# Sparse attention and a gated feed-forward on one core: at most three of the opening's transfers in flight

## The chip, the core and the metric

One NeuronCore of a Trainium2 chip runs the whole program. The metric is device time in microseconds (us) of one execution; the figure of record is the median of several runs. Times in a profile count from the start of its span.

## The reference

Attention over 8 batches, 8 heads, 576 positions and 64 values a head, then a feed-forward of 4608 tokens, 512 wide inside and out, 2048 hidden:

```python
mask_local = (rel >= 0) & (rel < 32)
mask_strided = (rel >= 0) & (pos[None, :] % 32 == pos[:, None] % 32)
scores = np.where(masks, q @ k.T / np.sqrt(D), -1e9)      # heads 0-3 local, 4-7 strided
attn = softmax(scores)
x = (attn @ v) laid out as (tokens, heads * D)
h = x @ w_in
sp = np.maximum(h, 0.0) + np.log1p(np.exp(-np.abs(h)))
g = h * erf(sp)
out = g @ w_out
```

## The kernel before

Inputs come in a layout made for the chip: for each batch and pair of heads one block of queries and keys (`qk_loc` or `qk_str`, for local and strided heads) and one of values (`v_loc`, `v_str`). The weights are of eight bytes a number and are loaded as pairs of 32-bit words (tile `words`, 512 KB a block of 128 by 512); VectorE joins the words to 32-bit floats in three steps (L628, L635, L641: `bits0`, `bits1`, `bits2`), ScalarE rounds them to a high part (L646) and VectorE keeps the rest (L649). There are 16 blocks of `w_in` and 16 of `w_out`. The feed-forward multiplies high and low parts (L678 into `h`, L750 into `o`), and its gate is worked out by ScalarE (L686) and VectorE (L683, L713, L719).

`heads` makes one pair of heads: two loads or more (L378 to L389), scores on TensorE (L400, and L413 adds the mask there), their maximum on VectorE (L436), the exponential on ScalarE, the sum and its inverse on VectorE (L481, L490, L491), the product on GpSimd (L498), a transpose on TensorE (L507) and the product with the values (L526). The eight pairs of the first two batches go first, and all but one of these borrow the space of weight blocks that come later (`home`), so their queries, keys and values are loaded in two parts, and those weight blocks are loaded when the pair is through. The other batches are made in between the feed-forward's work.

Nothing of the order is left to a scheduler. Each operation is an `Op` with an engine, a duration and a key; `Plan.order` plays them through and writes one fixed order for each engine, which `tc.keep_in_program_order` keeps. All loads and the first stores are issued by SyncE (engine `sp` in the plan), in that one order. The plan reckons with code fetches of TensorE, one in every 254 of its instructions:

```python
BLOCK, FIRST, FETCH = 254, 68, (4.0, 5.8)
late = max(0.0, fetched + self.FETCH[fetched < dma] - at)
```

The semaphores are put in by the framework: a transfer waits for its data's buffer to be free, and eight completion semaphores are used in turn, so that a transfer also waits for the landing of the eighth ahead of it.

The first 60 transfers of SyncE are: for the eight pairs of heads of the first two batches their loads, the masks (`con`) and the identity (`ident`), two loads of the third batch, and 30 of the 32 weight blocks, between 64 and 640 KB each. Numbers of transfers in this document count in the order of issue; 1 and 2 are the queries and keys of the first pair, 3 is `con`, 4 and 5 queries and keys of the second pair, 6 the first weight block, 7 and 8 values of the first pair (512 and 128 KB), 9 `ident`, 10 values of the second pair, 11 queries and keys of the third pair, 15 and 20 weight blocks of `w_in`.

Of the kernel before, what the change touches and what calls it, by code (L numbers as in the profile page):

```python
# [27 lines left out]

PRO = 36
SLOT = 4.6  # L30
BACKLOG = 1.1130116
FT = (31.6335, -135.614, 224.291, 52.3709, -149.741, 22.9733, 45.4447, 151.185, -55.3448, 2.76331, -71.5147, 15.0393)
KI = 6.0
# [124 lines left out]
class Plan:  # L158
# [14 lines left out]
    def add(self, eng, dur, key, emit, after=(), new=(), use=(), earliest=0.0):  # L173
        op = Op(eng, dur, key, emit, after, new, use, earliest)
        self.ops.append(op)
        return op
# [24 lines left out]
    def order(self):  # L201
# [5 lines left out]
        while left:  # L207
            best = None
            for e in self.ENGINES:
                can = [(o, n, self._ready(o, live)) for n, o in enumerate(queue[e][: self.WINDOW])]  # L210
                floor = max(free[e], dma - BACKLOG) if e == "sp" else free[e]
                port = held.get({"dve": "pool", "pool": "dve"}.get(e), 0.0)
# [54 lines left out]
def attention_moe(  # L267
# [39 lines left out]
    def buf(pool, tag, shape, name, dtype=F32):  # L307
        def make():
            return pools[pool].tile(shape, dtype, tag=tag, name=name, bufs=bufs[tag])

        return Buf(tag, make)
# [8 lines left out]
    def act(n, fixed=0.093):  # L320
        return fixed + n / 1200.0
# [343 lines left out]
    def ftile(k, c, f, first_f, last_f, ready):  # L665

        v0 = PRO + SLOT * k
        ph = buf("ps_h", "h", [P, 512], f"h_{k}")
# [73 lines left out]
        for t in range(NTT):  # L742
# [19 lines left out]
            if f == last_f:  # L762
# [12 lines left out]

                o = add("act", act(DM, 0.06), v0 + 2.5 * SLOT + 0.7 + 0.2 * t, evac, [o], [ob], [po])
                if first_f == 0:
# [30 lines left out]
    for f in range(0, DF, SW):  # L808
        for c in range(NCC):
            i = len(w1)  # L810
            rows, sl = slice(c * P, (c + 1) * P), slice(f, f + SW)
            op, pair = weight(i, w_in, rows, sl, KW[i // 8][i % 8])
            w1.append(op)
            win.append(pair)
    for f in range(NFC):
        rows, sl = slice(f * P, (f + 1) * P), slice(0, DM)
        op, pair = weight(NFC + f, w_out, rows, sl, KW[2 + f // 8][f % 8])
# [18 lines left out]
    for b in range(B):  # L836
        p2 = b // 2
        for i, hp in enumerate((0, 1, 2, 3)):
            keys = KP[4 * b + i]
            if p2 == 0:  # L840
                banks, home, act_sum, pool_norm = PAIRS[4 * b + i]
                done, o_s, o, loads = heads(
                    b, hp, keys, [], pe_mask=True, pool_norm=pool_norm, act_sum=act_sum, banks=banks, home=home, own=True
                )
# [22 lines left out]
    w, run = warm("o2")  # L867
    first = plan.add("pe", 0.217, -10.0, run, o_con, [w])
    plan.filler = (first, warm, ("o2", "o1", "o0", "ps"), mm1_first[6])
    for op in plan.order():  # L870
        for x in op.new:
            x.tile = x.make()
        for ins in op.emit():
            tc.keep_in_program_order(ins)


def _layout(q, k, v):
# [87 lines left out]
```

## Time and profile before

| | |
|---|---|
| median of 3 runs | 933.93 us (932.69 to 934.51) |
| the profiled execution | 933.05 us, span 931.3 us |
| busy: TensorE, VectorE, ScalarE, GpSimd | 909.7, 686.7, 653.4, 60.9 us |
| chain that ended last | TensorE 90%, VectorE 4%, ScalarE 3% |
| DMA, whole span | 68.86 MB, 74 GB/s |

PE is TensorE, PEld its weight loads, DVE VectorE, ACT ScalarE, POOL GpSimd, SPq the issue of transfers by SyncE. In a timeline row the first number is the start, the second the length; square brackets hold the idle time of the engine ahead of the instruction and what ended it, "issue" being nothing that the profile knows. In a row of busy times by stretch each engine has its busy us and the count of instructions (x), in the order PE, PEld, DVE, ACT, POOL, and then TensorE's granted clock, the DMA engines' busy share and their GB/s. Queue q1 carries SyncE's transfers, q8 and q14 carry code.

### The profile page before, as it was taken

To read this page: it belongs to the slowest core of one execution; us is meant where nothing else is said; L and a number is where in the kernel's file an instruction comes from. 1 tells how busy PE (TensorE), PEld (TensorE's weight loads), DVE (VectorE), ACT (ScalarE), POOL (GpSimd) and SP (SyncE) were. 2 spreads that over 40 slices of the span, in tenths; PEclk is the share of its full clock that TensorE was granted. 3 is DMA by queue.
4 is the path that set the end of the run, shared out by engine and by line. 5 is a ranking of instruction groups with operands and counts; after the bars stand their busy time and mean duration, and the time that the engine had idled before them with its cause. 6 is when DMAs were issued, how large, how long until landed. Compare 5 with 4: busy or idle time off the path is not lost.

```text
span 931.3 us, 20134 instructions
## 1 busy us (share of the span) xinstructions
PE 909.7 (98%) x8166; PEld 809.6 (87%) x8169; DVE 686.7 (74%) x1352; ACT 653.4 (70%) x1476; POOL 60.9 (7%) x59
## 2 busy tenths in 40 slices
PE   5789999999999999999999999999999999999998
PEld 4678888898888889988888899998898899999997
DVE  5999999996757766669886876667876666666664
ACT  5687887887776767667666666766766766766765
POOL 2200012110101100001110100000100000000000
PEclk9799999999999999999999999999999999999999
DMA  9994124321313010013312300002300200000000
GB/s 336 391 362 154 62 57 73 61 34 48 78 58 86 30 64 35 27 57 105 99 56 92 124 17 1 34 1 73 135 1 30 70 1 1 34 1 0 34 1 35
DMA packets 23421, 68.86 MB, mean 74 GB/s; under 512 B 2592, under 2 KB 3232, under 8 KB 23328
## 3 DMA queue, kind: packets, MB, share of 16 engines
q1 hardware_dynamic: 20736, 62.86, 18.9%
q0 software_dynamic: 2592, 4.72, 3.6%
q8 instruction: 64, 1.05, 0.5%
q14 instruction: 29, 0.24, 0.1%
HBM read 53.41 MB, written 14.16 MB: 73 GB/s over the span
## 4 chain that ended last, share of the span: by engine, by line
PE 90%; DVE 4%; ACT 3%; issue 1%; DMA 1%; SPq 0%; POOL 0%; ACTq 0%; POOLq 0%
PE h L678 41%; PE o L750 40%; PE s L400 3%; PE x L526 3%; PE t L507 2%; PE s L526 1%; DMA qk<-qk_loc 1%; ACT b L686 1%; DVE a L683 1%; DVE b L683 1%; ACT a L686 1%; PE s L507 1%; DVE glo L719 1%; ACT sm L472 0%; DVE h L713 0%
## 5 line engine op out<-in xcount | busy, mean ns | idle before, releaser
L750 PE MATMUL o<-pair,ghi 128*128 128x512 f32 x1152 | 361.4, 395 | 0.2 <-ACT ghi L716 0.2
L678 PE MATMUL h<-xhi,pair 128*128 128x384 f32 x1536 | 302.4, 339 | 0.6 <-DVE glo L719 0.6
L678 PEld LDWEIGHTS h<-xhi,pair 128*128 128x128 f32 x1536 | 271.4, 188 | 16.5 <-DVE glo L719 2.6
L686 ACT ACTIVATE b<-b 128x384 f32<-128x384 f32 x384 | 200.4, 522 | 77.2 <-DVE b L683 73.8
L750 PEld LDWEIGHTS o<-pair,ghi 128*128 128x128 f32 x1152 | 209.8, 188 | 32.4 <-ACT ghi L716 0.7
L750 PE MATMUL o<-pair,glo 128*128 128x512 f32 x576 | 224.8, 390 | 0.0
L683 DVE SCALAR_TENSOR_TENSOR a<-h,a 128x384 f32<-128x384 f32 x192 | 106.3, 553 | 83.3 <-ACT a L686 82.8
L678 PE MATMUL h<-xlo,pair 128*128 128x384 f32 x768 | 164.4, 336 | 0.0
L686 ACT ACTIVATE a<-h 128x384 f32<-128x384 f32 x192 | 93.5, 487 | 100.9 <-PE h L678 100.2
L683 DVE SCALAR_TENSOR_TENSOR a<-a,h 128x384 f32<-128x384 f32 x192 | 105.5, 549 | 68.9 <-ACT b L686 68.9
L713 DVE TENSOR_TENSOR h<-b,h 128x384 f32<-128x384 f32 x192 | 107.0, 557 | 46.2 <-ACT b L686 45.8
L678 PEld LDWEIGHTS h<-xlo,pair 128*128 128x128 f32 x768 | 136.0, 188 | 0.0
L750 PEld LDWEIGHTS o<-pair,glo 128*128 128x128 f32 x576 | 108.1, 188 | 23.7 <-DVE glo L719 0.3
L686 ACT ACTIVATE a<-a 128x384 f32<-128x384 f32 x192 | 100.3, 523 | 26.6 <-DVE a L683 26.1
L719 DVE TENSOR_TENSOR glo<-h,ghi 128x384 fp32r<-128x384 f32 x192 | 105.7, 550 | 11.7 <-ACT ghi L716 10.2
L716 ACT CAST ghi<-h 128x384 fp32r<-128x384 f32 x192 | 90.5, 471 | 29.1 <-DVE h L713 15.1
L683 DVE SCALAR_TENSOR_TENSOR b<-b,a 128x384 f32<-128x384 f32 x192 | 108.7, 566 | 1.0
L686 ACT ACTIVATE b<-a 128x384 f32<-128x384 f32 x192 | 101.0, 526 | 4.4
L498 POOL TENSOR_TENSOR sm<-sm,r 128x768 f32<-128x768 f32 (+3 forms) x36 | 45.0, 1249 | 435.3 <-DVE r L491 330.9
L436 DVE TENSOR_REDUCE mx<-s 128x12 f32<-128x768 f32 (+3 forms) x37 | 28.8, 784 | 10.6 <-PE s L413 10.3
L766 ACT COPY ob<-o 128x512 f32<-128x512 f32 x54 | 31.0, 588 | 2.7 <-PE o L750 2.2
L526 PEld LDWEIGHTS x<-pt,v 64*64 64x64 f32 x1392 | 24.4, 135 | 6.9 <-issue 4.4
(49 smaller groups left out, 511.4 us busy)
## 6 DMA issues: line engine op xcount, KB each, us to landing
out<-ob SPq DMA_DIRECT2D x36, 256.0 KB, 2.0
v<-v_loc SPq DMA_DIRECT2D x13, 640.0 KB, 4.1
words<-w_in SPq DMA_DIRECT2D x16, 512.0 KB, 8.6
words<-w_out SPq DMA_DIRECT2D x16, 512.0 KB, 9.1
qk<-qk_loc SPq DMA_DIRECT2D x13, 592.0 KB, 3.8
qk<-qk_str SPq DMA_DIRECT2D x12, 608.0 KB, 3.8
v<-v_str SPq DMA_DIRECT2D x16, 384.0 KB, 3.3
out<-ob POOLq DMA_DIRECT2D x18, 256.0 KB, 4.6
```

What stands on the lines that cost most here:

```text
L436: yield nc.vector.tensor_reduce(out=mx[:, parts[i], :units], in_=wide(of(s, i)), axis=mybir.AxisListType.X, op=ALU.max)
L498: yield (nc.gpsimd if pool_norm else nc.vector).tensor_tensor(out=d, in0=d, in1=spread(rc, i), op=ALU.mult)
L507: yield nc.tensor.transpose(bank(t, h)[:, 128 * w : 128 * w + 128], sm[:, h, c : c + 128], ident)
L526: yield nc.tensor.matmul(bank(px, m)[h * D : (h + 1) * D, a * n : (a + 1) * n], values(rows, (2 * a + h) * D), pt[rows, h, c : c + n], sta ...
L678: yield nc.tensor.matmul(ph[:, :CH], win[4 * s + cc][:, w, fs], x[cc][:, c0 : c0 + CH], start=(i == 0), stop=(i == len(terms) - 1))
L683: yield nc.vector.scalar_tensor_tensor(out=out, in0=in0, scalar=scalar, in1=in1, op0=op0, op1=op1)
L686: yield nc.scalar.activation(dst, src, func, bias=bias[i], scale=scale)
L713: yield nc.vector.tensor_tensor(out=ph[:, :CH], in0=bb.tile, in1=ph[:, :CH], op=ALU.mult)
L716: yield nc.scalar.copy(ghi.tile, ph[:, :CH])
L719: yield nc.vector.tensor_tensor(out=glo.tile, in0=ph[:, :CH], in1=ghi.tile.bitcast(F32), op=ALU.subtract)
L750: yield nc.tensor.matmul(po.tile, g[:, ts], wout[f][:, w], start=(f == first_f and i == 0), stop=(f == last_f and i == 2),)
L766: yield nc.scalar.copy(ob.tile, po.tile)
```

## The change

In the loop that emits the planned order, the first 60 operations of SyncE are noted as they come; each from the fourth on gets a dependency on the transfer three places ahead, of the kind that waits for its data to have landed. The order of every engine, the buffers and all computation stay as they were.

```diff
+AHEAD = 3
+NLOADS = 60
...
+    loads, landed = [], mybir.DependencyInfo(mybir.DependencyClass.Sync, mybir.DependencyReason.DATA)
     for op in plan.order():
         for x in op.new:
             x.tile = x.make()
         for ins in op.emit():
             tc.keep_in_program_order(ins)
+            if op.eng == "sp" and len(loads) < NLOADS:
+                loads.append(ins.ins)
+                if len(loads) > AHEAD:
+                    tc.add_manual_dep(ins.ins, loads[-1 - AHEAD].name, landed, reason="transfers ahead")
```

## The prediction

> **What bounds the kernel now.** I read the page first, then its DMA view for the first 70 us (40 slices of 1.75), busy times by stretch, the chain of waits over the first 150 us, SyncE's own timeline, and the DMA and count views of single stretches.
>
> ```profile
> span 931.3 us, 20134 instructions
> DMA  0999999999999999999999999999999999999638
> GB/s 0 283 274 332 296 372 424 406 393 414 394 380 395 388 401 323 352 394 413 400 402 403 393 395 399 403 404 408 414 400 409 412 412 412 405 413 389 272 94 241
> ```
>
> The DMA engines are full from 1.75 us until 65: after a slow first 10 us (274 to 372 GB/s) they move some 400 GB/s without a hole. Nearly all 60 transfers of the change lie in that stretch. The profiled execution took 933.05 us, 1.75 more than its span and 0.88 under the median of the three runs shown (933.93); I work in differences and add them to the median.
>
> ```profile
> 109.00:137.00 28.00, 27.37 (x138) 24.20 (x137) 28.00 (x57) 23.01 (x50) 1.91 (x2) 1.00 0.18 40
> 137.00:931.00 794.00, 790.11 (x6554) 708.53 (x6552) 564.45 (x1093) 552.85 (x1187) 46.92 (x40) 1.00 0.16 47
> ```
>
> Behind 137 us TensorE (first busy column) is idle 3.9 of 794 us, between 109 and 137 us VectorE (third) is idle never. There is no slack to swallow a shift: what the opening gains or loses by some 30 us is kept to the end, since the order on every engine is fixed. So the opening decides. Its chain of waits (start, length, what):
>
> ```profile
> 5.83 9.20 DMA qk<-qk_loc
> 15.07 1.04 PE s L400 x64
> 20.29 1.92 issue
> 25.55 3.12 issue
> 32.16 0.82 DVE mx L436
> ```
>
> A load of queries and keys issued at 5.83 lands at 15.03 and holds TensorE; then TensorE stands 1.92 and 3.12 us for nothing that the semaphores show. Those two are code fetches. Counts of matmuls (TensorE's column) and weight loads (the next) from the start to these two stops, and to 836.02:
>
> ```profile
> 0.00:20.31 20.31, 12.89 (x347) 8.65 (x349) 10.16 (x28) 9.61 (x45) 3.95 (x9) 1.00 0.92 329
> 0.00:25.56 25.56, 16.17 (x474) 10.93 (x476) 15.03 (x40) 13.84 (x59) 5.48 (x10) 1.00 0.94 342
> 0.00:836.02 836.02, 818.25 (x7710) 727.53 (x7713) 631.62 (x1245) 591.37 (x1341) 60.90 (x59) 0.99 0.25 80
> ```
>
> 347 and 474: 127 matmuls apart, so I read the program as coming in blocks of 127 matmuls with their weight loads, of which the next isn't there yet; 836.02 is 58 blocks behind 347 by the weight loads (7713). The queue views say what holds it (packets, MB, share); the rows are those of 15.80:19.65, 19.65:20.80, 22.20:26.13 and 26.13:27.30, then 491.38:495.08 and 495.08:496.10, then 836.02:836.74 and 836.74:837.70:
>
> ```profile
> q1 hardware_dynamic: 503, 1.55, 103.4%
> ...
> q8 instruction: 1, 0.02, 6.1%
> ...
> q1 hardware_dynamic: 613, 1.53, 103.1%
> ...
> q8 instruction: 1, 0.02, 6.0%
> ...
> q1 hardware_dynamic: 140, 0.66, 48.6%
> ...
> q8 instruction: 1, 0.02, 5.7%
> ...
> DMA packets 0, 0.00 MB, mean 0 GB/s; under 512 B 0, under 2 KB 0, under 8 KB 0
> ...
> q8 instruction: 1, 0.02, 6.2%
> ```
>
> A code packet appears only at the start of the second window of each pair. TensorE enters a block at 15.8 (matmul 220), 22.21, about 491.4 (4919) and 836.02 (7713); the packet starts 3.9, 3.9, 3.7 and 0.7 us later. With the load stream full it waits 3.9, with one 640 KB load in flight 3.7, with none 0.7. The packet takes 1.1 us, and TensorE goes on 1.4 us behind it (20.8 to 22.21, 27.25 to 28.66).
>
> **The change part by part.** SyncE's timeline (start, length; in order these are transfers 8 to 11, 14 to 16, 19 and 28):
>
> ```profile
> 4.01 0.54 SPq L389 DMA_DIRECT2D qk<-v_loc  x1
> 4.60 0.71 SPq L790 DMA_DIRECT2D ident<-ident_f  x1
> 5.35 0.43 SPq L386 DMA_DIRECT2D v<-v_str  x1
> 5.83 0.74 SPq L378 DMA_DIRECT2D qk<-qk_loc  x1
> ...
> 9.71 0.33 SPq L381 DMA_DIRECT2D qk<-qk_str  x1
> 11.26 0.33 SPq L622 DMA_DIRECT2D words<-w_in  x1
> 11.64 1.21 SPq L386 DMA_DIRECT2D v<-v_loc  x1
> ...
> 15.05 0.33 SPq L386 DMA_DIRECT2D v<-v_str  x1
> ...
> 24.62 0.33 SPq L389 DMA_DIRECT2D qk<-v_loc  x1
> ```
>
> *What is removed.* From the ninth on, SyncE already waits: transfer 14 goes out at 9.71, 15 at 11.26, 16 at 11.64, 19 at 15.05, on the landings of the eighth ahead (6, 7, 8, 11). Eight in flight become three. The wait for the third covers the wait for the eighth, so no instruction is added on balance: nothing, and 0.02 us to wake (19 at 15.05 on a landing at 15.03).
>
> *What the wait costs the stream.* A load that goes out when the engines have drained pays a fixed part. Transfers by kind (KB, median us to landing); the first three kinds go out alone for the most part, the last two are transfers 8 and 9:
>
> ```profile
> qk<-qk_loc SPq DMA_DIRECT2D x13, 592.0 KB, 3.8
> v<-v_str SPq DMA_DIRECT2D x16, 384.0 KB, 3.3
> out<-ob SPq DMA_DIRECT2D x36, 256.0 KB, 2.0
> qk<-v_loc SPq DMA_DIRECT2D x3, 128.0 KB, 7.6
> ident<-ident_f SPq DMA_DIRECT2D x1, 64.0 KB, 7.2
> ```
>
> At 412 GB/s, 592 KB are 1.47 us and 384 KB 0.95, so 2.3 is fixed for a load; 256 KB are 0.64, so 1.4 for a store. In the stream the fixed part lies beside the two transfers still in flight. Two of 512 KB (1.27 each, 2.54) cover 2.3. Two of 304 KB (1.5) cover it only if the engines never drain. I take no loss there, since a stream that hasn't drained is nearer to the 1.4; the other end goes to a rival. One place drains surely: transfers 8 and 9 hold 128 and 64 KB, 0.5 us together, and 10 waits for 7. It goes out at 11.26, lands 2.3 + 0.95 later at 14.5 instead of 13.6: 0.9 us late (bounds 0, if it is as short as a store's, and 1.8, if the code packet of that moment isn't hidden in the hole). Transfer 11, the load TensorE waits for, lands 0.9 late. All later ones keep the 0.9.
>
> *Who feels it.* VectorE's timeline:
>
> ```profile
> 19.24 0.43 DVE L628 TENSOR_SCALAR w<-words 128x512 uint32<-128x512 uint32 x1 [0.70 <-DMA words<-w_in]
> ...
> 26.11 0.42 DVE L628 TENSOR_SCALAR w<-words 128x512 uint32<-128x512 uint32 x1
> 29.54 0.49 DVE L436 TENSOR_REDUCE mx<-s 128x5 f32<-128x320 f32 x1 [1.54 <-PE s L413]
> ```
>
> Transfer 15 (a weight block) is waited for at 19.24: 0.9 late moves VectorE's queue from there, so that it is through at 28.9 instead of 28.0, still before the maximum at 29.54, for which it waits 1.54 us on TensorE (29.54 - 1.54 = 28.0). Transfer 20 lands at 24.6 and is used at 26.11: covered. (It landed when 28, the eighth behind it, went out.) The waits of weight loads for TensorE and ScalarE stand in the same queue; the landing waits now end later than those. Stores lie behind transfer 62 and don't change.
>
> *What the code fetch gains.* Three in flight leave less ahead of the code packet than eight. The bounds are 0.7 and 3.9 us; one load alone gave 3.7, so I take a modest 3.3. Then: TensorE starts at 15.97 instead of 15.07, enters the block at 16.7, the packet starts at 20.0, TensorE goes on at 20.0 + 1.1 + 1.4 = 22.5 (was 22.21); the next packet starts at 25.8 and TensorE goes on at 28.3 (was 28.66). The maximum on VectorE starts 0.3 earlier, at 29.2, and VectorE is free for it at 28.9.
>
> **Sum:** +0.9 at the first load, partly taken up in the first fetch stop, -0.3 behind the second: 933.93 - 0.3 = 933.6 us.
>
> **The rivals.** *The code packet waits as long as before.* One lone load already makes 3.7 of the 3.9, which speaks for it; that a lone load starts slowly, against. Then the 0.9 of the first load goes through both fetch stops: 934.8 us. The Trainium skill, "DMA: Bandwidth & Descriptors", section "Queues, rings and completion order", has it that an engine takes turns between queues and finishes the packet of descriptors it has begun; by that rule the depth behind that packet is of no account, as in this rival, and the trace so far agrees (3.7 beside 3.9).
>
> *Slower: three can't fill the stream.* If the fixed part counts in the stream as it does for lone loads, every transfer behind two short ones stalls: 10 most, then 15 (behind two of 304 KB), 19, 20, 23 and 26. Taking each landing as the later of the one before and the third ahead plus the fixed part, plus its own time, transfer 26 comes 3.7 us late with 2.1 and 5.5 late with 2.4. It landed at 31.3 (transfer 34 went out on it), and VectorE unpacks it as the second of this pair, near 34.4:
>
> ```profile
> 31.32 0.33 SPq L622 DMA_DIRECT2D words<-w_out  x1
> 34.06 1.26 DVE L628 TENSOR_SCALAR w<-words 128x512 uint32<-128x512 uint32 x2
> ```
>
> That is 3.0 of margin, and 5.5 late stops VectorE, which has no idle time left from there on, for 2.5: 936.4 us. It decides from a fixed part of about 2.1 on; lone loads show 2.3, and against it stands that the stream isn't cold.
>
> *Faster: the fetch falls near its undisturbed 0.7.* Then VectorE is the limit: it can gain no more than its 1.54 us of waiting before 29.54, if transfer 15 isn't late either: 932.4 us.
>
> *The wait does nothing,* because landings in order imply it: 933.9 us. Against it: 10 and 11 went out at 5.35 and 5.83, long before 7 and 8 had landed.
>
> **How the numbers follow.** Forecast 0.37; fetch unchanged 0.28; stream not filled 0.2; fetch much shorter 0.12; no effect 0.03. The first two differ by 1.2 us and both lie within 0.2% (1.9 us, about what a measurement of this kernel tells from no change). The likeliest alone spans 932.6 to 934.6. The range reaches to the limit of the fast case, with 0.5 us for the scatter of the three runs, and nearly to the slow one: 932.0 to 936.2. Faster by over 0.2%: 0.08, the fast case with VectorE's small gaps closed too; slower: 0.22, the slow case and part of the unchanged fetch; within: 0.70.
>
> **What would show it.** In the changed kernel transfer 4 goes out at 3.6 rather than 2.1, and each later one just behind the landing of the third ahead; 10 and 11 land near 14.5 and 15.9; TensorE's wait for that load ends near 15.97; the two stops near 21.2 and 25.9 are 1.3 and 2.4 us. If code packets still start 3.9 us into a block, the first rival holds; if the rate from 15 to 60 us falls under 380 GB/s, the second. Wrong it would also be if VectorE came later than 28.9 to its maximum, or a load behind 20 were late for its use.

## Result and profile after

| kernel | median, us | ratio to before, 95% interval |
|---|---|---|
| before (4 runs) | 933.31 | |
| after (4 runs) | 954.38 (953.77 to 954.56) | 1.0222 (1.0206 to 1.0239) |

The change costs 21 us, 2.2%, where 933.6 and at most 936.2 were forecast. The span of the profiled execution is 952.0 us, before 931.3. From the page of the changed kernel the span and the DMA engines in 40 slices of the span; then the DMA line of the page of before; then busy times by stretch:

```profile
span 952.0 us, 20131 instructions
DMA  7788322332133211003321310001300200000000
GB/s 239 254 281 312 132 93 34 60 60 34 47 75 90 79 35 61 27 1 115 89 103 51 127 52 1 34 1 51 124 29 8 89 1 1 34 0 1 34 1 34
```

```profile
DMA  9994124321313010013312300002300200000000
```

```profile
15.00:60.00 45.00, 29.98 (x781) 24.78 (x782) 34.37 (x83) 25.80 (x107) 8.09 (x8) 0.73 0.83 265
```

```profile
15.00:60.00 45.00, 36.16 (x861) 29.32 (x863) 40.61 (x97) 32.47 (x131) 10.04 (x10) 0.85 1.03 397
```

The first of the two stretches is the changed kernel's, the second the same 45 us of before (TensorE's clock, the DMA engines' busy share and GB/s are its last three numbers): the stream falls from 397 to 265 GB/s, with the engines 0.83 busy. Where before the DMA slices were full up to the third, they are now 7 or 8 tenths up to the fourth. TensorE's granted clock in these 45 us differs too, 0.73 beside 0.85; what that does to the time isn't separated here, but it goes down to 0.77 in a kernel below that loses 5 us only, and is 0.81 in one that loses 9.8.

SyncE's timeline of the changed kernel (transfers 4, 10, 11, 20 and 28, then 59 to 62 in one row and the first three stores in another), and the row of these stores in the kernel before:

```profile
3.59 0.33 SPq L382 DMA_DIRECT2D qk<-qk_str  x1
...
11.58 0.33 SPq L388 DMA_DIRECT2D v<-v_str  x1
11.96 0.85 SPq L380 DMA_DIRECT2D qk<-qk_loc  x1
...
26.93 0.33 SPq L624 DMA_DIRECT2D words<-w_in  x1
...
38.74 0.33 SPq L391 DMA_DIRECT2D qk<-v_loc  x1
...
91.71 2.85 SPq L624 DMA_DIRECT2D words<-w_out  x4
94.62 2.34 SPq L771 DMA_DIRECT2D out<-ob  x3
```

```profile
80.35 2.74 SPq L769 DMA_DIRECT2D out<-ob  x3
```

Transfer 28 goes out 14.1 us later than before (38.74, was 24.62), and the stores of the first results, which went out from 80.35 on before, go out from 94.62. What the engines wait for (us in total, times, longest), in the first 110 us on VectorE and the first 70 on TensorE:

```profile
DVE mx L438 <- PE s L415: 12.8, 3, 7.1
DVE w L630 <- DMA words<-w_in: 8.9, 5, 2.9
DVE w L630 <- DMA out<-ob: 8.9, 1, 8.9
```

```profile
PE s L509 <- POOL sm L500: 7.0, 3, 5.3
PE s L402 <- DMA qk<-qk_loc: 6.7, 3, 3.3
PE s L402 <- DMA qk<-qk_str: 3.8, 1, 3.8
```

Two things are new. Loads are waited for (weights, queries and keys), and VectorE stands once for 8.9 us on a *store*. In its timeline:

```profile
42.00 0.43 DVE L630 TENSOR_SCALAR w<-words 128x512 uint32<-128x512 uint32 x1 [2.76 <-DMA words<-w_in]
...
103.49 0.43 DVE L630 TENSOR_SCALAR w<-words 128x512 uint32<-128x512 uint32 x1 [8.93 <-DMA out<-ob]
```

The first row is transfer 26: it lands 10.7 us late (42.0, before 31.3). The second unpacks a weight block into a buffer that it shares with the results (`ob`): it can't start before a stored result has left. The same instruction in the kernel before started at 84.55 without a wait. In the chain of waits of the changed kernel ScalarE makes the first two results in one row (L768), and the store takes 8.77 us, issue to landing, against 2.0 for a store alone. It went out behind four loads still in flight, of which the last landed at 102.60:

```profile
89.67 1.08 ACT ob L768 x2
...
94.62 8.77 DMA out<-ob
103.39 0.03 issue
```

The store lands 21 us later than before (103.39, was 82.43), and this has three parts. Its data is ready at 90.26, before at 80.33: 9.9 us late, because everything ahead is. SyncE comes to it 4.4 us after that, where before it was there at once. And the loads ahead make it 6.7 us longer (8.77, was 2.08).

By instruction, matched in the fixed order of TensorE, the changed kernel is 6.6 us behind at 50 us of before, 10 behind at 60 and still at 84, and 20.7 behind at 92 and at the end.

### The profile page after: what moved, and what is told of

It is laid out like the page before. It is cut to its first block, busy times and chain, and to the rows that moved or that the text cites. A ratio compares the mean times of both kernels' runs of the same rounds, so it can differ in the third digit from the quotient of the medians.

```text
span 952.0 us, 20131 instructions
## 1 busy us (share of the span) xinstructions
PE 914.5 (96%) x8166; PEld 813.6 (85%) x8169; DVE 687.2 (72%) x1352; ACT 653.9 (69%) x1476; POOL 61.0 (6%) x59
## 4 chain that ended last, share of the span: by engine, by line
PE 82%; DVE 7%; DMA 7%; ACT 2%; issue 1%; SPq 0%; DVEq 0%; ACTq 0%
PE h L680 38%; PE o L752 37%; PE x L528 3%; DMA words<-w_in 2%; PE s L402 2%; PE t L509 2%; DVE a L685 2%; DMA qk<-qk_loc 1%; DVE b L685 1%; DVE glo L721 1%; DMA out<-ob 1%; ACT b L688 1%; DMA v<-v_loc 1%; DVE h L715 1%; DMA qk<-qk_str 1%
## 5 line engine op out<-in xcount | busy, mean ns | idle before, releaser
L721 DVE TENSOR_TENSOR glo<-h,ghi 128x384 fp32r<-128x384 f32 x192 | 105.8, 551 | 11.7 <-ACT ghi L718 10.2
L768 ACT COPY ob<-o 128x512 f32<-128x512 f32 x54 | 31.0, 589 | 3.0 <-PE o L752 2.4
L402 PEld LDWEIGHTS s<-qk 64*32 64x32 f32 (+1 forms) x1616 | 21.2, 118 | 11.5 <-DMA qk<-qk_loc 3.7
```

The lines of the kernel that those rows point to most:

```text
L402: yield nc.tensor.matmul(bank(s, h)[m * j : m * (j + 1), 64 * t : 64 * (t + 1)], queries(rows, q0, m), keys_of(rows, q0), start=(h, j) not ...
L721: yield nc.vector.tensor_tensor(out=glo.tile, in0=ph[:, :CH], in1=ghi.tile.bitcast(F32), op=ALU.subtract)
L768: yield nc.scalar.copy(ob.tile, po.tile)
```

## The experiments

Each kernel's ratio is to runs of the kernel before on the same chip (medians 932.8 to 932.9 there).

| kernel | median, us | ratio, 95% interval |
|---|---|---|
| four in flight | 937.61 | 1.0058 (1.0037 to 1.0079) |
| five | 932.77 | 0.9996 (0.9987 to 1.0006) |
| six | 933.04 | 0.9999 (0.9988 to 1.0009) |
| three, stores by ScalarE | 945.63 | 1.0128 (1.0113 to 1.0144) |
| three, transfers 1 to 28 only | 940.75 | 1.0084 (1.0069 to 1.0099) |
| three, transfers 29 to 60 only | 942.68 | 1.0105 (1.0081 to 1.0129) |
| the same, stores by ScalarE | 934.58 | 1.0022 (1.0012 to 1.0032) |
| before, stores by ScalarE | 932.87 | 1.0001 (0.9992 to 1.0011) |
| halves by partitions, six in flight | 974.75 | 1.0448 (1.0430 to 1.0465) |
| halves by columns, six in flight | 951.71 | 1.0190 (1.0173 to 1.0207) |
| halves by columns, eight in flight | 937.90 | 1.0049 (1.0030 to 1.0069) |

**How many in flight.** The limit is set to four, and in two more kernels to five and to six.

```diff
-AHEAD = 3
+AHEAD = 4
```

> Four in flight instead of three, all else as in the changed kernel (954.4 us). Theory A, drained engines: with three in flight a 512 KB load lands about 5.1 us after its issue though the three need only 3.8 of pure moving, because the DMA engines run empty between landing and the next issue and start slowly again; four need 5.1, so they just about fill that time. Then landing 60 falls from 99.6 to 78-82 us (before: 74.2) and most of both losses goes: 934 to 940 us. Theory B, every step of narrowing costs alike (SyncE's waiting itself): a fifth of the loss goes, 949 to 951 us.

> Five in flight. Theory A: the stream is full as before, loads land within 1-2 us of before, while less stands ahead of TensorE's code packets (in the changed kernel they started 1.3 to 1.5 us into a block in the first 32 us, before 3.9): 931.5 to 934.5 us. Theory B: 945 us.

> Six in flight. Theory A: as before in the loads, code packets between the two, 932 to 934 us. Theory B: 940 us.

The loss falls from 21 us to 5 with four and to nothing with five. Theory B, a like price for every step, is out, and theory A holds. The hoped-for gain of a shorter queue in front of the code packets can't be measured in the times with five or six. The same 45 us with four, five and six in flight, one row each:

```profile
15.00:60.00 45.00, 33.55 (x852) 27.99 (x854) 38.55 (x93) 30.28 (x127) 9.84 (x10) 0.85 0.92 316
```

```profile
15.00:60.00 45.00, 34.41 (x852) 27.52 (x839) 42.39 (x101) 33.74 (x134) 10.02 (x10) 0.89 1.00 367
```

```profile
15.00:60.00 45.00, 36.81 (x857) 29.86 (x860) 39.47 (x93) 31.70 (x129) 10.04 (x10) 0.81 1.00 376
```

316, 367, 376 GB/s against 265 with three and 397 with eight. So the rate itself rises step by step; it is the time that stops falling, as soon as the loads are early enough for who waits for them.

**The loads by themselves.** All computation is left out of this kernel and zeros are written for the result; SyncE loads weight blocks in stretches with a set number in flight:

```diff
+            if len(made) > depth:
+                tc.add_manual_dep(ins.ins, made[-1 - depth].name, landed, reason="ahead")
...
+    phase(lambda dst, src: nc.sync.dma_start(dst, src), 3, 16, 1024)
```

The last line is one stretch: three in flight, 16 loads of 1024 words a partition (512 KB).

> Loads alone: all of the attention and the feed-forward is left out, and zeros are written for the result. 512 KB weight blocks are loaded with 8, 1, 2, 3, 4, 5, 6 and 8 in flight, then 288 KB parts of them with 3, 5 and 8, each stretch behind the landing of the one ahead of it. Theory C, my prediction's rule (the fixed 2.3 us lies beside the others in flight): us per 512 KB load 3.6, 1.8, 1.27 and 1.27 from four on, for one, two, three and more in flight; 288 KB with three 1.0, with five 0.71. Theory A (engines that ran empty start slowly, as the changed kernel suggests, 5.1 us for three): 3.6, 2.2 to 2.5, 1.6 to 1.8, 1.3 to 1.4, 1.27; 288 KB with three 1.2 or more, with five 0.8. If three in flight give 1.27 here, the slow stream needs the other work beside it.

The stretches with 1, 2, 3, 4 and 5 in flight, 512 KB each, and 288 KB with 3 and 5 (the last three columns: TensorE's clock, busy share of the DMA engines, GB/s):

```profile
23.90:51.70 27.80, 0.00 (x0) 1.00 0.48 151
51.70:78.30 26.60, 0.00 (x0) 1.00 0.72 237
78.40:107.00 28.60, 0.00 (x0) 1.00 0.85 293
107.00:130.30 23.30, 0.00 (x0) 1.00 0.92 360
130.30:153.60 23.30, 0.00 (x0) 1.00 0.92 360
199.60:219.70 20.10, 0.00 (x0) 1.00 0.73 235
219.80:236.90 17.10, 0.00 (x0) 1.00 0.82 276
```

These are means with the start and end of each stretch, from one execution. From landing to landing, without the first three of a stretch, a 512 KB load takes 3.47, 2.16, 1.70, 1.33 and 1.27 us with one to five in flight, and 1.27 with six and eight. A 288 KB load takes 1.17, 0.83 and 0.74 us with three, five and eight, where its own moving at the full rate is 0.71. Theory A's numbers hold to within 4%, my prediction's (1.8 with two, 1.27 with three) don't, and no other work is needed to make the stream slow. It shows how it is slow: with three in flight the engines are busy 0.85 at 293 GB/s, full 0.92 at 360. So part of the loss is idle time (0.85 beside 0.92) and part is slower moving while busy (345 GB/s per busy share, against 391). The slower moving is that of a few packets: the median 4 KB packet takes 159 ns in both stretches, but 6.7% of them take over 250 ns with three in flight and 1.9% with five. With one in flight, where it can be told apart, 90 of the 106 such packets begin within 0.6 us of their transfer's first. That is what theory A calls a slow start.

**Bytes or count.**

```diff
-AHEAD = 3
-NLOADS = 60
+AHEAD = 6
+NLOADS = 120
...
+    def two(dst, src):
+        yield nc.sync.dma_start(dst[:64], src[:64])
+        yield nc.sync.dma_start(dst[64:], src[64:])
...
-                yield nc.sync.dma_start(qk[0][:, : wq + S + 32], src)
+                yield from two(qk[0][:, : wq + S + 32], src)
```

Every other load is cut in two in the same way.

> Every load in two halves of 64 partitions each, limit six in flight for the first 120: the same bytes in flight as in the changed kernel, twice the count. Theory A (bytes in flight too few for the engines' restart): the stream is as slow as in the changed kernel, landing of the last near 99 us, 950 to 958 us. Theory B (the number in flight or the waits of SyncE matter, not bytes): like six in flight, 932 to 942 us.

It came out worse than both theories:

```profile
15.00:60.00 45.00, 25.75 (x646) 20.27 (x648) 29.52 (x72) 22.63 (x92) 9.95 (x10) 0.66 0.92 225
```

225 GB/s with engines 0.92 busy: the halves themselves move slowly (a 4 KB packet of these 45 us takes 267 ns in the median, 160 in the kernel before), so the trial says nothing on bytes or count. The Trainium skill, "SBUF — State Buffer", section "Door 1: The DMA port swizzle", has it that 64 neighbouring partitions reach only half of the ports through which DMA writes; by that rule such a half alone would move at half the rate, an estimate. The 225 beside 397 go that way, but lower and upper halves were in flight together, and no other run here tests it. The cut was then made by columns, all 128 partitions in each half:

```diff
+        n = dst.shape[-1] // 2
+        yield nc.sync.dma_start(dst[:, :n], src[:, :n])
+        yield nc.sync.dma_start(dst[:, n:], src[:, n:])
```

For eight halves the added limit is left out (`NLOADS = 0`), and the eight semaphores alone hold the transfers.

> Every load in two halves by columns (128 partitions each), six in flight for the first 120: the bytes in flight of the changed kernel with twice the count. It mends the trial by halves of partitions, where each half may use but a part of the memory's width (225 GB/s with the DMA engines 0.92 busy). Theory A (bytes in flight count): like the changed kernel, 950 to 960 us. Theory B (the count matters): like six in flight, 932 to 938 us.

> The same halves by columns without the added limit, so eight halves in flight by the semaphores: the bytes of four whole transfers. Theory A: like four in flight, 936 to 943 us. Theory B: like eight, 932 to 935 us.

Six halves cost nearly what three wholes cost (951.7 beside 954.4), eight halves what four wholes cost (937.9 beside 937.6). The rates agree, 276 GB/s beside 265 and 319 beside 316:

```profile
15.00:60.00 45.00, 30.63 (x782) 25.51 (x782) 35.28 (x84) 26.93 (x112) 8.69 (x9) 0.73 0.88 276
```

```profile
15.00:60.00 45.00, 36.12 (x854) 29.12 (x854) 39.63 (x94) 31.30 (x129) 10.25 (x11) 0.77 0.97 319
```

So bytes in flight count far more than the number of transfers or SyncE's waits. That halving costs something by itself isn't excluded, as no run has halves with more bytes in flight. Nor is it bytes alone: in the kernel of loads five of 288 KB (1.4 MB) move 357 GB/s and three of 512 KB (1.5 MB) 308.

**Where the 21 us are lost.** First the early part of the limit by itself (first edit), and the late part (second edit):

```diff
-NLOADS = 60
+NLOADS = 28
```

```diff
-                if len(loads) > AHEAD:
+                if len(loads) > 28:
```

> Three in flight for the first 28 transfers only. Theory: the loads up to 28 come about 10 us late as in the changed kernel, VectorE and TensorE lose that, then the stream fills again at 400 GB/s and no store waits: 941 to 945 us. Rival, the early lateness is made good later by slack behind 30 us: 934 to 937 us.

> Three in flight for transfers 29 to 60 only. Theory: these loads have 6 to 100 us of margin before, so no load is waited for, but SyncE comes to the first stores some 4 to 8 us late and they land behind loads: 936 to 942 us with one stop of VectorE at a weight unpacking near 84 us, that waits for a store. Rival, all of the loss is the early loads': 933 to 934 us.

The early part alone costs 7.8 us (940.75 - 932.92), the late part alone 9.8 (its four runs scatter from 940.1 to 945.6). VectorE's waits in the first 110 us, early part alone, and its one long stop with the late part alone:

```profile
DVE w L630 <- DMA words<-w_in: 8.1, 4, 2.5
```

```profile
90.51 0.43 DVE L630 TENSOR_SCALAR w<-words 128x512 uint32<-128x512 uint32 x1 [7.72 <-DMA out<-ob]
```

So they are different losses: late loads in the first, the store in the second. Then the first three stores were taken out of SyncE's queue, so that they go out right behind the copies that make their data:

```diff
-                    yield nc.sync.dma_start(out[...], ob.tile)
+                    yield (nc.scalar if c == 0 else nc.sync).dma_start(out[...], ob.tile)
```

> The changed kernel with its first three stores of the result (transfers 63 to 65) issued by ScalarE's queue right behind the copies that they store, instead of by SyncE behind the 60 waiting loads. Theory: about 9 of the 21 us lost are those stores: they went out at 94.6 and landed at 103.4 behind loads, and VectorE, which needs the store's buffer for the next weight block, stood 8.9 us. Then 944 to 947 us, with VectorE's 8.9 us stop gone. Rival: the stop only takes up what the late loads had cost anyway (the weights would be late too), 953 to 955 us.

> Three in flight for transfers 29 to 60 only, and the first three stores issued by ScalarE's queue. Theory: the late limit cost 9.8 us by the stores alone (VectorE stood 7.7 us for one), so nothing is left: 932 to 935 us. Rival, late loads count too: 936 to 939 us.

> The kernel before, with the first three stores issued by ScalarE's queue. Control: before, no one waits for these stores, so 932 to 935 us. If ScalarE pays for the issue, up to 1 us more.

In the changed kernel this gives back 8.8 us (954.4 to 945.6), with the late part alone 8.1 (942.7 to 934.6); in the kernel before it changes nothing. The stops of VectorE that are left at that instruction, changed kernel and late part alone:

```profile
96.77 0.43 DVE L630 TENSOR_SCALAR w<-words 128x512 uint32<-128x512 uint32 x1 [1.60 <-DMA out<-ob]
```

```profile
84.55 0.43 DVE L630 TENSOR_SCALAR w<-words 128x512 uint32<-128x512 uint32 x1 [1.35 <-DMA out<-ob]
```

What is left of the late part, 1.7 us, is about this stop: ScalarE issues the store at 78.73, and it still takes 5.7 us to land. The sum: 21.1 us in all, less 8.8 for the stores (954.4 - 945.6) and 7.8 for the early loads, leaves 4.5 us, of which the late part has 1.7 by itself; some 3 us are in neither part alone. The changed kernel's 3.8 us wait of TensorE on a `qk_str` load, transfer 39, is of that size; in the late part alone its longest wait for such a load is 1.0. The order of TensorE puts them at this place: the changed kernel falls from 6.6 to 10 us behind between 50 and 60 us of before, where it waits for transfer 39, and the early part alone stays at 6.7. So the lateness of the early and of the late loads adds up there; no run takes this wait away by itself.

## Why the prediction was wrong

**The step that failed first** is "Two of 512 KB (1.27 each, 2.54) cover 2.3", and with it "I take no loss there". It treats the fixed part as mere waiting that runs beside the two transfers in flight. Measured alone, three of 512 KB take 1.70 us each, not 1.27; it takes five to reach 1.27. In the kernel, transfer 10 came as worked out (out at 11.58, 11.26 forecast; landed at 14.46, 14.5 forecast), but 11 landed at 17.7 and not 15.9, and the lateness grew from there: 26 was 10.7 us late, where I had 0.9, and 5.5 in the slow rival.

That rival, "three can't fill the stream", is the mechanism that came, with a chance of 0.2, and its fixed part was too small. By its rule 1.70 us a load with three in flight means a fixed part of 3.8 us (3 times 1.70, less the 1.27 of moving), where lone loads had given 2.3 (3.47 less 1.27 is 2.2). In the same way it is 3.0 with two of 512 KB in flight and 2.8 with three of 288 KB, so it is no constant and grows with the bytes in flight. Worked through again on the landings of the kernel before, the rule makes transfer 26 late by 4.2 us with 2.4 (not the 5.5 of the prediction, and 2.7, not 3.7, with 2.1), by 6.2 with 2.8 and by 11.7 with 3.8. These are estimates from the runs, and the 10.7 measured lies between the last two. With 2.4 the rule also gives no loss behind two of 512 KB. Rates behind a landing are the thing to measure, not lone latencies less the moving time.

**The second** is "Stores lie behind transfer 62 and don't change". They change in three ways: their data is 9.9 us late, SyncE, which works in order, is held by its waits for landings 4.4 us longer, and the data of the last loads lies ahead of theirs, which makes 6.7 us. I named what is queued behind the waiting loads, and left out who waits for it: VectorE, through the buffer `ob` that weight blocks and results share. Its stop for the store is 8 to 9 of the 21 us.

**The code fetch** came out better than forecast and bought nothing. In the changed kernel TensorE is at matmul 347 at 23.85 and 473 at 29.95 (counts in brackets), and the code packets start after 25.21 and 31.15:

```profile
0.00:23.85 23.85, 13.89 (x347) 0.93 0.78 239
0.00:29.95 29.95, 17.60 (x473) 0.91 0.79 245
```

```profile
q1 hardware_dynamic: 182, 0.51, 89.0%
...
q8 instruction: 1, 0.02, 5.7%
...
q1 hardware_dynamic: 144, 0.38, 82.8%
...
q8 instruction: 1, 0.02, 5.8%
```

The four rows are those of 23.80:25.21, 25.21:26.20, 29.90:31.15 and 31.15:32.10. That is 1.4 and 1.2 us into a block, where before it was 3.9 and I took 3.3, and TensorE's two stops for code are gone: its row at the first place has no idle time.

```profile
23.27 0.93 PE L402 MATMUL s<-qk,qk 64*64 64x64 f32 x48
```

TensorE waited for loads instead, and for longer (10.5 us for queries and keys in the first 70). The three code packets behind matmuls 220, 347 and 474, which the kernel before gets 3.8, 3.9 and 3.7 us into a block, came after 4.0, 4.2 and 3.7 with six in flight, 3.7, 2.8 and 5.3 with five, 3.4, 2.0 and 5.4 with four, and 1.4, 1.4 and 1.2 with three (one execution each). So only three in flight made them come early throughout, in a stream that had drained to 0.8 busy. By the rule of turns between queues in the Trainium skill, "DMA: Bandwidth & Descriptors", section "Queues, rings and completion order", which the prediction cites, the depth should not have mattered. Six against eight agree with it. Three against eight don't, though the engines were then also idle for a part of the time, so these runs don't tell the two apart. Why one lone load of 640 KB held the packet for 3.7 us and three in flight for 1.4 stays open.

**Right** were that the waits themselves cost nothing to issue (mostly 16 to 17 ns from a landing to the next issue, at most 0.09 us; 20131 instructions for 20134), that behind 137 us nothing swallows a shift, and that SyncE's third-ahead wait does what it says (transfer 4 out at 3.59, 3.6 forecast).

## What to carry to other kernels

A limit on transfers in flight is above all a limit on bytes in flight: before setting one, measure the rate at that depth with the real sizes, since a lone transfer's latency doesn't tell it. Here 512 KB loads needed five (2.5 MB) to be at their full rate and four for nearly that. And a wait put into an in-order queue delays everything behind it: follow each later instruction of that queue to whoever waits for it, through shared buffers too. Before blaming the queue, see when the instruction's data was ready.

## What the runs showed of the hardware

- Rate against depth, loads alone, one execution: 512 KB takes 3.47, 2.16, 1.70, 1.33 and 1.27 us with one to five in flight, and 288 KB 1.17, 0.83 and 0.74 with three, five and eight. Of the twelve spacings behind the 0.83, ten are 0.70 to 0.79; two long ones make the difference to eight.
- With few loads in flight the DMA engines are not only idle at times but slower while busy, 345 against 391 GB/s per busy share at three and at five in flight, by a few slow packets (over 250 ns beside a median of 159), which with lone loads come mostly at a transfer's start.
- Loads cut into halves of 64 partitions moved 225 GB/s with engines 0.92 busy; as halves by columns, 128 partitions each, they moved 276 with 0.88, and the kernel was 23 us faster.
- A 256 KB store that went out behind four 512 KB loads of the same queue took 8.77 us to land, and 2.0 alone.
